# Moving three inverse transforms and their products to other places of a long-convolution and gated-MLP gradient kernel

## The chip, the core and the metric

The kernel runs on one core of one Trainium2 chip. The core has a matrix engine (PE), a vector engine (DVE), a scalar engine (ACT), a general engine (POOL), and a sequencer (SP) that here only issues DMAs; DMAs are issued from SP and from POOL. The metric is the device time of one execution in microseconds.

## The reference

The reference computes a forward pass and the gradients of all its inputs; ten arrays come out. S = 2048 rows, D = 1024 columns, F = 3584, all bf16. Cut to what matters:

```python
def _A_ref(q, k, v, shift_k, ssm_k, ssm_D):        # q is layernorm(x)
    k_shift = sum(k_pad[:, t:t + S] * shift_k[:, 3 - t] for t in range(4))
    kv = k_shift * v
    y = irfft(rfft(kv, 2 * S) * rfft(ssm_k, 2 * S))[:S]   # per column
    return q * (y + kv * ssm_D)

def _B_ref(x, w_gate, w_up, w_down):
    return ((x @ w_gate) * (x @ w_up)) @ w_down

xn = layernorm(x)
out = x + _A_ref(xn, k, v, shift_k, ssm_k, ssm_D) * silu(_B_ref(xn, ...))
# and the gradients of q, k, v, shift_k, ssm_k, ssm_D, w_gate, w_up, w_down
```

The gradient needs the same convolution theorem twice more: with DY the gradient at y, the gradient of kv is the inverse transform of P1 = F(DY) times conj(F(ssm_k)), and the gradient of ssm_k is that of P2 = F(DY) times conj(F(kv)).

## The kernel before

The kernel is written with a tile framework: the code names tiles of pools, and the framework puts in all waits and fixes, when the program is built, the order of instructions on each engine and each DMA queue. It goes by the order of the code as a priority and by a modelled time, so an instruction that is later in the code can be placed ahead of one that the model still sees waiting. On the chip each engine then runs its list strictly in that order. Pools of SBUF are stacked: a pool opened after another was closed takes over its addresses, and a tile of it waits until the last user of those addresses is done. `nc.any.tensor_copy` is put on ACT or DVE by the framework. `dma()` alternates between SP and POOL.

The Fourier transforms are matrix products with twiddle tables of 1024 x 1024 cosines and sines (`twc`, `tws`, held in HBM as TWd and loaded in eight rows of 128 x 1024). Rows of a sequence are split by parity (`sigma` or `par`), columns in two halves (`dh`) of 512. A forward transform (`fwd_transform2`, L226) takes 8 frequency blocks (`gb`), two parities, two halves, and for each 16 matmuls of 128x512 into two PSUM tiles `psA` and `psB`; ACT copies them to SBUF. A spectrum consists of an even part E, an odd part O and, for two of the three, the odd part rotated by a phase (`rotate_O`, L264, four DVE instructions). Products of spectra (`cprod2`, L288) make real and imaginary parts by `csum4` (L272): four multiplications (L278), two sums (L283, L285), and a final sum (L286), each over 128x512 bf16. The two `cprod2` of one (gb, dh) item thus are 28 instructions, of which the imaginary part of the second (7, tag "j") goes to POOL through `eng_i=nc.gpsimd` and 21 to DVE. An inverse transform (`inv_transform2`, L246) takes 8 row blocks (`ub`), two parities and two halves, each 16 matmuls (L256) and one of a single row (L259) into `psI`, and hands the tile to a callback.

The stages in the order of the code, with their tiles:

- H: twiddle tables are made, ssm_k is transposed and transformed, with layer norm and the shifted k beside it; spectra HF go to HBM.
- KV: forward transform of kv (tile KVs), products Y = KVF x HF into the tile YS (64 KB a partition), KVF to HBM (`kv_on_acc`, L475). Y inverse with callback `y_on_out` (L523): writes YFULLd and SOUTd.
- Gate/up: WD is loaded, xn transposed to XNT, then g, u and h = g*u for 28 blocks of F (L551 to L588), written to GTd, UTd, HTd.
- BM: h times w_down, silu and its gradient, writes the output, DYd, DXNAd, DBMd.
- DY: forward transform of DY (`dy_on_acc`, L684), products P1 into the tile YS2, DYF to HBM. Inverse 1 with callback `dkv_on_out` (L741; tiles cb, dyD, dkv, dksh, dv) and, after each of its 8 row blocks, `p2_task` (L765): it loads DYF and KVF, scales DYF on ACT (L774), makes P2 and stores it to HBM. Then P2 is loaded back into YS2, and inverse 2 with `dh_on_out` (L806) transposes its result into DSSMK.
- DBMT: DBM transposed; FG (L839 to L882): for 7 groups of 4 blocks of F, `ps_dh` matmuls, products dgt and dut on DVE, their transposes, then two sets of `ps_dw` matmuls for the weight gradients.
- DWD (L927 to L963): gradient of w_down on PE, with `dk_block` (L888) beside it, which makes the gradients of k and of shift_k on DVE.
- dx (L969 to L1032): gate and up weights transposed (`pst_wt`), then 16 row blocks for each half of D with 56 matmuls `ps_dxn` each; the first half is kept in HALF (f32), the second goes on through the layer-norm gradient.

Of the kernel before, what the change touches and what calls it, by code (L numbers as in the profile page):

```python
# [17 lines left out]
def build_kernel(  # L18
# [71 lines left out]
    DYFd = dram.tile([NB2, P, 4 * D], BF16, name="DYFd")  # L90
    P2d = dram.tile([NB2, P, 4 * D], BF16, name="P2d")
# [217 lines left out]

    def transpose_blocks(pspool, srcs, dst_fn, nblk, tagname):  # L310
# [143 lines left out]

    with tc.tile_pool(name="kvpool", bufs=1) as kvpool, \
            tc.tile_pool(name="twpool_f", bufs=2) as twpool, \
            tc.tile_pool(name="nrows_f", bufs=1) as nrf, \
            tc.tile_pool(name="yspool_f", bufs=1) as yspool:
# [8 lines left out]
        YS = yspool.tile([P, NB2, 2, 2, D], BF16, name="YS")  # L467
        with tc.tile_pool(name="kvf_sb", bufs=2) as kfs, \
                tc.tile_pool(name="kvf_tmp", bufs=1) as ktmp, \
# [5 lines left out]
            def kv_on_acc(sigma, gb, dh, psA, psB):  # L475
                if gb not in kvf_tiles:
                    kvf_tiles[gb] = kfs.tile([P, 3, 2, D], BF16, name="kvf_t")
                    hf_in[gb] = kfs.tile([P, 3, 2, D], BF16, name="hf_in")
                    dma(hf_in[gb][:].rearrange("p a c d -> p (a c d)"), HFd[gb])
                kt = kvf_tiles[gb]  # L480
                ht = hf_in[gb]
# [3 lines left out]
                if sigma == 1:  # L485
                    rotate_O(kt[:, 2, 0, sl], kt[:, 2, 1, sl], kt[:, 1, 0, sl], kt[:, 1, 1, sl], gb, ktmp)
                    Ek = (kt[:, 0, 0, sl], kt[:, 0, 1, sl])
                    Ok = (kt[:, 1, 0, sl], kt[:, 1, 1, sl])
                    Eh = (ht[:, 0, 0, sl], ht[:, 0, 1, sl])
                    Oh = (ht[:, 1, 0, sl], ht[:, 1, 1, sl])  # L490
                    Orh = (ht[:, 2, 0, sl], ht[:, 2, 1, sl])
                    cprod2(YS[:, gb, 0, 0, sl], YS[:, gb, 0, 1, sl], Ek, Eh, False, Ok, Orh, False, ktmp, "yp")
                    cprod2(YS[:, gb, 1, 0, sl], YS[:, gb, 1, 1, sl], Ek, Oh, False, Ok, Eh, False, ktmp, "yp", eng_i=nc.gpsimd)
                    if dh == DH - 1:
                        dma(KVFd[gb], kt[:].rearrange("p a c d -> p (a c d)"))
                        del kvf_tiles[gb]
                        del hf_in[gb]

            def kv_on_nyq(sigma, dh, psN):
                sl = slice(dh * 512, (dh + 1) * 512)  # L500
                nc.scalar.copy(out=KNb[0:1, sigma, sl], in_=psN[:])
                if sigma == 1:
# [10 lines left out]
                    if dh == DH - 1:  # L513
                        nc.sync.dma_start(out=KVFNd[:, :], in_=KNb[:].rearrange("o s d -> o (s d)"))

            fwd_transform2(KVs, lambda b: load_tw_row(twpool, b), fps, kv_on_acc, kv_on_nyq)

        with tc.tile_pool(name="yi_sb", bufs=3) as ysb, \
                tc.tile_pool(name="yi_xn", bufs=2) as yxn, \
                tc.tile_pool(name="ips", bufs=2, space=bass.MemoryType.PSUM) as ips:  # L520
            xn_tiles = {}

            def y_on_out(par, ub, dh, ps):  # L523
                key = (par, ub)
                if dh == 0:
                    xn_tiles[key] = yxn.tile([P, D], BF16, name="xn_l")
                    dma(xn_tiles[key][:], par_rows(XNd, par, ub))
                sl = slice(dh * 512, (dh + 1) * 512)
                yb = ysb.tile([P, 512], BF16, name="yb")
                nc.scalar.copy(out=yb[:], in_=ps[:])  # L530
                kvD = ysb.tile([P, 512], BF16, name="kvD")
                nc.vector.tensor_tensor(kvD[:], KVs[:, par, ub, sl], Dbc[:, sl], ALU.mult)
                yfull = ysb.tile([P, 512], BF16, name="yfull")
                nc.vector.tensor_tensor(yfull[:], yb[:], kvD[:], ALU.add)
                dma(par_rows(YFULLd, par, ub, sl), yfull[:])
                sout = ysb.tile([P, 512], BF16, name="sout")
                nc.vector.tensor_tensor(sout[:], xn_tiles[key][:, sl], yfull[:], ALU.mult)
                dma(par_rows(SOUTd, par, ub, sl), sout[:])
                if dh == DH - 1:
                    del xn_tiles[key]  # L540

            inv_transform2(YS, YN, lambda b: load_tw_row(twpool, b), ips, y_on_out)

    twbase.release()

    wdp = tc.alloc_tile_pool(name="wd_pool", bufs=1, side="right")
    WD = wdp.tile([P, FC, D], BF16, name="WD")
    for fc in range(FC):
        dma(WD[:, fc, :], B_w_down[fc * P:(fc + 1) * P, :])

    with tc.tile_pool(name="xnt_pool", bufs=1) as xtp:  # L551
# [9 lines left out]
        with tc.tile_pool(name="wslab", bufs=2) as wsl, \  # L561
                tc.tile_pool(name="gu_sb", bufs=3) as gus, \
                tc.tile_pool(name="gu_ps", bufs=2, space=bass.MemoryType.PSUM) as gps:
            for fg in range(FG):
# [4 lines left out]
                for fi in range(4):  # L569
                    fc = fg * 4 + fi  # L570
                    for sq in range(SQ):
# [16 lines left out]
                        dma(HTd[rs, cs], h_b[:])  # L588

# [71 lines left out]
    with tc.tile_pool(name="yspool_b", bufs=1) as yspool, \  # L661
            tc.tile_pool(name="nrows_b", bufs=1) as nrb, \
            tc.tile_pool(name="twpool_b", bufs=2) as twpool:
        YS = yspool.tile([P, NB2, 2, 2, D], BF16, name="YS2")
        YN = nrb.tile([1, 2, D], BF16, name="YNb")
        dypool = tc.alloc_tile_pool(name="dypool", bufs=1)
# [4 lines left out]
        with tc.tile_pool(name="dyf_sb", bufs=2) as dfs, \  # L671
# [431 lines left out]
```

## Time and profile before

| quantity | value |
| --- | --- |
| median of 4 runs | 3579.45 us (3576.46 to 3580.23) |
| profiled execution, its own time | 3576.46 us |
| span of the profiled execution | 3574.7 us |
| mean granted PE clock | 0.893 of full speed |
| moved by DMA over the span | 582.86 MB, 163 GB/s |
| PE idle in the KV stage until ACT has copied `kvf_t` | 91.4 us |

The span runs from the first to the last instruction; what lies around it is 1.8 us. Busy time is the time in which at least one instruction of an engine runs. Matmuls are pipelined: one lasts 379 ns, but the next starts well before its end, so PE's pace is read from starts or from a whole stage. The table of stages gives busy time, the granted clock and the DMA traffic for stretches of the span; the starts of stages in it are read from the first and last matmul of each PSUM tile. A line such as L256 or L278 is that of a helper that several stages share; the tiles named beside it tell the stages apart.

### The profile page before, as it was taken

What the parts mean: (1) busy time and instruction counts of PE and PEld (TensorE: products, weight loads), DVE (VectorE), ACT (ScalarE), POOL (GpSimd) and SP (SyncE); (2) the same over time, 40 slices, a digit from 0 to 9 for tenths busy, and PEclk for the clock granted to TensorE, in tenths of its full rate; (3) what the DMA queues carried; (4) which work ended last, traced back from release to release, by engine and by line L of the source; (5) the groups of instructions that cost most, each with busy time, mean ns of one, the idle gap of its engine ahead of it and who ended that gap; (6) DMA issues with size and microseconds to landing.
All of it is one profiled execution on the core that took longest, in us unless ns stands there. A gap on an engine that the chain in (4) does not pass through costs nothing. (4 is left out here: it accounts for less than half of the span.)

```text
span 3574.7 us, 39595 instructions
## 1 busy us (share of the span) xinstructions
PE 2834.9 (79%) x13811; PEld 1299.8 (36%) x14074; DVE 1528.6 (43%) x3373; ACT 1086.4 (30%) x2849; POOL 1091.9 (31%) x1281
## 2 busy tenths in 40 slices
PE   5945459699999976454444969999999899699798
PEld 2412224344443322121111444444444344444443
DVE  7979973111115547686663032222222651100244
ACT  6411101433321111111111454444444444510432
POOL 2237742122232329866662010010010220011021
PEclk9977779799999988777766979999999999799799
DMA  7773254443447742333444063333342873455486
GB/s 268 285 256 121 88 196 144 143 161 139 162 146 244 265 177 89 106 121 141 158 174 170 30 240 116 110 114 121 119 127 99 298 247 124 152 144 160 140 242 183
DMA packets 327911, 582.86 MB, mean 163 GB/s; under 512 B 144655, under 2 KB 195855, under 8 KB 318236
## 3 DMA queue, kind: packets, MB, share of 16 engines
q1 hardware_dynamic: 250350, 292.42, 25.3%
q0 software_dynamic: 77360, 287.89, 22.3%
q8 instruction: 110, 1.80, 0.2%
q14 instruction: 91, 0.75, 0.1%
HBM read 379.62 MB, written 204.77 MB: 163 GB/s over the span
## 5 line engine op out<-in xcount | busy, mean ns | idle before, releaser
L256 PE MATMUL psI<-YS,twc_t 128*128 128x512 bf16 x754 | 309.5, 411 | 266.1 <-ACT cb L750 156.4
L1000 PE MATMUL ps_dxn<-WGT,dgt_l 128*128 128x512 bf16 x890 | 338.4, 380 | 1.8
L577 PE MATMUL psU<-XNT,wu_s 128*128 128x512 bf16 x888 | 337.8, 380 | 1.5
L576 PE MATMUL psG<-XNT,wg_s 128*128 128x512 bf16 x868 | 330.6, 381 | 9.1 <-DMA wg_s<-in_B_w_gate_dram 5.3
L1000 PE MATMUL ps_dxn<-WUT,dut_l 128*128 128x512 bf16 x862 | 327.6, 380 | 0.6 <-ACT WUT L317 0.4
L256 PE MATMUL psI<-YS,tws_t 128*128 128x512 bf16 x748 | 304.1, 407 | 8.4 <-DVE YS L286 7.3
L877 PEld LDWEIGHTS <-XNR 128*128 128x128 bf16 x1792 | 174.4, 98 | 206.9 <-issue 2.0
L862 PE MATMUL ps_dh<-DBMT,WDT 128*128 128x512 bf16 x861 | 205.9, 380 | 4.6 <-ACT DBMT L317 2.6
L256 PEld LDWEIGHTS <-tws_t 128*128 128x128 bf16 x768 | 79.1, 103 | 347.4 <-issue 280.7
L955 PE MATMUL ps_dwd<-DBM,HH 128*128 128x512 bf16 x868 | 202.2, 380 | 3.1 <-ACT wd_b L960 0.8
L608 PE MATMUL ps_bm<-WD,ht_t 128*128 128x512 bf16 x877 | 195.5, 379 | 5.8 <-DMA ht_t<-HTd 4.8
L583 DVE TENSOR_TENSOR h_b<-g_b,u_b 128x512 bf16<-128x512 bf16 x112 | 47.6, 425 | 352.1 <-ACT u_b L581 352.1
L877 PE MATMUL ps_dw<-DG,XNR 128*128 128x512 bf16 x875 | 196.2, 379 | 2.3 <-ACT DG L317 1.2
L877 PE MATMUL ps_dw<-DU,XNR 128*128 128x512 bf16 x879 | 193.6, 379 | 0.9
L242 PE MATMUL psA<-KV,twc_t 128*128 128x512 bf16 x245 | 100.4, 413 | 91.4 <-ACT kvf_t L483 91.4
L880 ACT CAST w_b<-ps_dw 128x512 bf16<-128x512 f32 x112 | 65.6, 585 | 295.1 <-PE ps_dw L877 292.2
L317 DVE COPY WDT<-pst_fg 128x128 bf16<-128x128 bf16 x81 | 17.9, 224 | 316.9 <-PE pst_fg L315 309.3
L579 ACT CAST g_b<-psG 128x512 bf16<-128x512 f32 x112 | 65.5, 585 | 276.4 <-PE psG L576 266.8
L278 POOL TENSOR_TENSOR p1j_m<-da_t,hf_in 128x512 bf16<-128x512 bf16 x64 | 139.9, 2206 | 26.3 <-ACT da_t L692 13.7
L243 PE MATMUL psB<-DY,tws_t 128*128 128x512 bf16 x256 | 102.3, 400 | 55.7 <-DMA tws_t<-TWd 54.2
L68 POOL DMA_DIRECT2D out_dram<-w_b x56 | 30.4, 542 | 361.1 <-ACT w_b L880 316.4
L608 PEld LDWEIGHTS <-ht_t 128*128 128x128 bf16 x896 | 86.0, 98 | 121.6 <-issue 15.7
(332 smaller groups left out, 5299.2 us busy)
## 6 DMA issues: line engine op xcount, KB each, us to landing
dgt_l<-DGTd SPq DMA_DIRECT2D x32, 896.0 KB, 5.6
dut_l<-DUTd POOLq DMA_DIRECT2D x32, 896.0 KB, 8.4
hf_in<-HFd SPq DMA_DIRECT2D x16, 1536.0 KB, 7.4
kt<-KPAD SPq DMA_DIRECT2D x64, 256.0 KB, 5.4
kt<-KPAD POOLq DMA_DIRECT2D x64, 256.0 KB, 5.7
ut_t<-UTd POOLq DMA_DIRECT2D x28, 512.0 KB, 7.2
gt_t<-GTd SPq DMA_DIRECT2D x28, 512.0 KB, 5.7
DGTd<-dgt SPq DMA_DIRECT2D x28, 512.0 KB, 3.0
```

The costliest lines, as they stand in the source:

```text
L242: nc.tensor.matmul(psA[:], twc_t[:, ub * P:(ub + 1) * P], rhs, start=(ub == 0), stop=(ub == NB2 - 1))
L243: nc.tensor.matmul(psB[:], tws_t[:, ub * P:(ub + 1) * P], rhs, start=(ub == 0), stop=(ub == NB2 - 1))
L256: nc.tensor.matmul(ps[:], tws2[c][:, gb * P:(gb + 1) * P], Pspec[:, gb, par, c, dh * 512:(dh + 1) * 512], start=first, stop=False)
L278: e.tensor_tensor(m[:], a, b, ALU.mult)
L576: nc.tensor.matmul(psG[:], wg_s[:, dc, fi * P:(fi + 1) * P], rhs, start=(dc == 0), stop=(dc == DC - 1))
L577: nc.tensor.matmul(psU[:], wu_s[:, dc, fi * P:(fi + 1) * P], rhs, start=(dc == 0), stop=(dc == DC - 1))
L608: nc.tensor.matmul(ps[:, dh * 512:(dh + 1) * 512], lhsT, WD[:, fc, dh * 512:(dh + 1) * 512], start=(fc == 0), stop=(fc == FC - 1))
L862: nc.tensor.matmul(ps[:], WDT[:, ddc, fi * P:(fi + 1) * P], DBMT[:, ddc, cs], start=(ddc == 0), stop=(ddc == DC - 1))
L877: nc.tensor.matmul(ps[:], XNR[:, sb, dc * P:(dc + 1) * P], src[:, sb, :], start=(sb == 0), stop=(sb == NB - 1))
L880: nc.scalar.copy(out=w_b[:], in_=ps[:])
L955: nc.tensor.matmul(pss[k][:, dh * 512:(dh + 1) * 512], HH[:, sb, fi * P:(fi + 1) * P], DBM[:, sb, dh * 512:(dh + 1) * 512], start=(sb == 0 ...
L1000: nc.tensor.matmul(ps[:], lt[:, fc, :], wt[:, fc, :], start=(i_acc == 0), stop=(i_acc == n_acc - 1))
```

## The change

- KV: products are no longer split; all 28 instructions of an item run on DVE (`eng_i` isn't given any more). They go to a small tile `ystg` and from there to HBM (Yd). `GB_IN = NB2` makes this hold for all 8 blocks, so that the list of Y items for the gate/up stage (`y_items`) is empty.
- The Y inverse runs after gate/up and before BM. WD is loaded after gate/up in the code, just ahead of it. The callback loads its part of xn and kv itself.
- DY: the forward transform only copies and stores DYF; no HF is loaded. XNR is loaded ahead of DY in the code.
- P1: 16 items (`product_pass_item`), each two loads, 28 DVE instructions and a store, are placed by `p1_tick` along the 28 blocks of FG. Inverse 1 follows FG; DBM is loaded after it in the code.
- P2: 16 items, with the scaling on ACT, are placed by `p2_tick` along the 32 row blocks of dx; inverse 2 comes last in the kernel. HALF becomes bf16.
- The inverses are `inv_transform2h`: the half `dh` is the outer loop, a half of the spectrum is loaded from HBM (tile YSh, two buffers), and all twiddle rows are loaded once for each half.
- DBM's pool no longer overlaps in time with that of DBMT and XNR.

The core of the diff:

```diff
+    def y_products(dst2, kt3, ht3, pool, tag):
...
+        cprod2(dst2[:, 0, 0, :], dst2[:, 0, 1, :], Ek, Eh, False, Ok, Orh, False, pool, tag)
+        cprod2(dst2[:, 1, 0, :], dst2[:, 1, 1, :], Ek, Oh, False, Ok, Eh, False, pool, tag)
...
+    def product_pass_item(kind, gb, dh, io_pool, tmp_pool):
+        sl = slice(dh * 512, (dh + 1) * 512)
+        out_t = io_pool.tile([P, 2, 2, 512], BF16, name=f"pp_out_{kind}")
...
+        elif kind == "P1":
+            dt = io_pool.tile([P, 2, 2, 512], BF16, name="pp_dyf")
+            dma(dt[:], DYFv[gb, :, :, :, sl])
+            ht = io_pool.tile([P, 3, 2, 512], BF16, name="pp_hf")
+            dma(ht[:], HFv[gb, :, :, :, sl])
+            p1_products(out_t, dt, ht, tmp_pool, "pp1")
+            dma(P1v[gb, :, :, :, sl], out_t[:])
...
+    def make_pass_scheduler(kind, io_pool, tmp_pool, total_slots):
+        items = [(gb, dh) for gb in range(NB2) for dh in range(DH)]
...
+        def tick(i, final=False):
+            target = len(items) if final else min(len(items), (len(items) * (i + 1) + total_slots - 1) // total_slots)
+            while state["done"] < target:
...
+    def inv_transform2h(Psrc_v, PNsrc, tw_pool, ys_pool, nr_pool, pspool, on_out, side_task=None):
...
+        for dh in range(DH):
+            sl = slice(dh * 512, (dh + 1) * 512)
+            first_tw = load_tw_row(tw_pool, 0)
+            YSh = ys_pool.tile([P, NB2, 2, 2, 512], BF16, name="YSh")
+            for gb in range(NB2):
+                dma(YSh[:, gb, :, :, :], Psrc_v[gb, :, :, :, sl])
+            for ub in range(NB2):
+                twc_t, tws_t = first_tw if ub == 0 else load_tw_row(tw_pool, ub)
...
+                for par in range(2):
...
+                    on_out(par, ub, dh, ps)
...
-                    cprod2(YS[:, gb, 0, 0, sl], YS[:, gb, 0, 1, sl], Ek, Eh, False, Ok, Orh, False, ktmp, "yp")
-                    cprod2(YS[:, gb, 1, 0, sl], YS[:, gb, 1, 1, sl], Ek, Oh, False, Ok, Eh, False, ktmp, "yp", eng_i=nc.gpsimd)
+                    if gb < GB_IN:
+                        ht = hf_in[gb]
+                        ystg = yst.tile([P, 2, 2, 512], BF16, name="ystg")
+                        y_products(ystg, kt[:, :, :, sl], ht[:, :, :, sl], ktmp, "yp")
+                        dma(Ydv[gb, :, :, :, sl], ystg[:])
...
-            inv_transform2(YS, YN, lambda b: load_tw_row(twpool, b), ips, y_on_out)
...
+        inv_transform2h(Ydv, YNd, ytw, yys, ynr, ips, y_on_out)
...
-                    cprod2(YS[:, gb, 0, 0, sl], YS[:, gb, 0, 1, sl], Ed, Eh, True, Od, Oh, True, dtmp, "p1")
-                    cprod2(YS[:, gb, 1, 0, sl], YS[:, gb, 1, 1, sl], Ed, Orh, True, Od, Eh, True, dtmp, "p1", eng_i=nc.gpsimd)
...
-            inv_transform2(YS, YN, lambda b: load_tw_row(twpool, b), ips, dkv_on_out, side_task=p2_task)
...
-            inv_transform2(YS, YN, lambda b: load_tw_row(twpool, b), ips, dh_on_out)
...
+            p1_tick = make_pass_scheduler("P1", p1io, p1tmp, FG * 4)
...
+                    p1_tick(fg * 4 + fi)
...
+        inv_transform2h(P1v, P1Nd, i1tw, i1ys, i1nr, ips, dkv_on_out)
...
-        HALF = hfp.tile([P, NB, 512 * max(DH - 1, 1)], F32, name="HALF")
+        HALF = hfp.tile([P, NB, 512 * max(DH - 1, 1)], BF16, name="HALF")
+        p2_tick = make_pass_scheduler("P2", p2io, p2tmp, DH * NB)
...
+                p2_tick(dh * NB + sb)
...
+        inv_transform2h(P2v, P2Nd, i2tw, i2ys, i2nr, ips, dh_on_out)
```

More of the change, by code (lines that the diff above doesn't have):

```diff
@@ L496, in kv_on_acc @@
                         del kvf_tiles[gb]
-                        del hf_in[gb]
+                        if gb in hf_in:
+                            del hf_in[gb]
             def kv_on_nyq(sigma, dh, psN):
```

404 lines of the change are left out of this document (225 added, 179 removed).

## The prediction

> **What bounds the kernel now.** I read the page first, then busy time by stage, then who waits for whom, then single instructions in order of time.
>
> ```profile
> span 3574.7 us, 39595 instructions
> PE 2834.9 (79%) x13811; PEld 1299.8 (36%) x14074; DVE 1528.6 (43%) x3373; ACT 1086.4 (30%) x2849; POOL 1091.9 (31%) x1281
> PE   5945459699999976454444969999999899699798
> ```
>
> The span lies 1.8 us under this execution's own 3576.46 us; the median of the runs is 3 us above that. No engine is full over the whole span. PE is at 9 tenths in most of the 40 slices and at 4 to 6 in two valleys, slices 3 to 6 and 16 to 22, counted from 1. The table of stages puts names to them (columns: us, PE, PEld, DVE, ACT and POOL busy with counts, granted PE clock, DMA share, GB/s):
>
> ```profile
> 65.00:190.00 125.00, 116.45 (x518) 51.65 (x527) 116.93 (x319) 66.72 (x122) 33.53 (x56) 0.99 0.81 292
> 246.00:467.00 221.00, 125.24 (x501) 53.07 (x511) 219.35 (x332) 33.55 (x64) 163.93 (x112) 0.78 0.30 110
> 467.00:507.00 40.00, 10.35 (x34) 3.36 (x34) 40.00 (x75) 0.75 (x2) 19.22 (x17) 0.61 0.24 92
> 507.00:628.00 121.00, 118.68 (x504) 48.13 (x514) 37.82 (x98) 18.62 (x32) 32.26 (x60) 0.97 0.55 194
> 628.00:664.00 36.00, 14.86 (x128) 11.24 (x125) 7.87 (x35) 24.60 (x95) 6.08 (x10) 0.57 0.42 131
> 664.00:1060.00 396.00, 387.50 (x1756) 175.87 (x1792) 47.60 (x112) 120.25 (x224) 95.77 (x174) 0.99 0.40 147
> 1060.00:1298.00 238.00, 222.69 (x937) 89.76 (x956) 121.64 (x182) 34.39 (x33) 71.72 (x134) 1.00 0.69 236
> 1298.00:1328.00 30.00, 12.71 (x29) 2.92 (x30) 7.48 (x13) 2.16 (x4) 6.40 (x12) 0.60 0.82 303
> 1328.00:1533.00 205.00, 122.27 (x509) 52.44 (x519) 159.02 (x292) 34.85 (x66) 184.15 (x110) 0.80 0.27 96
> 1533.00:1567.00 34.00, 5.29 (x17) 1.58 (x16) 34.00 (x52) 0.17 (x1) 20.36 (x19) 0.62 0.20 78
> 1567.00:1872.00 305.00, 147.26 (x519) 56.33 (x529) 207.47 (x436) 47.24 (x60) 192.76 (x162) 0.73 0.44 154
> 1872.00:1936.00 64.00, 10.95 (x27) 3.69 (x27) 30.35 (x50) 4.27 (x4) 26.64 (x30) 0.55 0.64 246
> 1936.00:2067.00 131.00, 126.92 (x631) 55.35 (x643) 0.61 (x2) 55.94 (x155) 4.86 (x9) 0.97 0.11 37
> 2067.00:2112.00 45.00, 18.39 (x145) 14.43 (x146) 10.40 (x49) 25.13 (x99) 11.20 (x21) 0.53 0.86 323
> 2112.00:2784.00 672.00, 653.82 (x3719) 322.91 (x3790) 174.09 (x620) 296.72 (x933) 65.99 (x123) 1.00 0.36 117
> 2784.00:3075.00 291.00, 269.05 (x1460) 118.89 (x1489) 120.90 (x215) 140.36 (x451) 54.19 (x100) 0.98 0.59 211
> 3104.00:3340.00 236.00, 214.92 (x1080) 107.15 (x1098) 16.42 (x69) 45.31 (x159) 26.99 (x20) 0.92 0.55 154
> 3374.00:3564.00 190.00, 188.60 (x861) 85.73 (x876) 80.46 (x105) 53.20 (x76) 37.83 (x43) 1.00 0.73 215
> ```
>
> In order these are: H forward transform, KV forward with the Y products (two rows), Y inverse, XNT transposes, gate/up matmuls, BM, the DY boundary, DY forward with the P1 products, their tail, inverse 1 with the P2 products, reload of P2, inverse 2, DBMT transposes, FG, DWD, and the two halves of dx. FG, gate/up, BM and dx are full of PE work. The valleys are the product stages: there DVE is busy throughout (219 of 221) or POOL is (184 of 205, 193 of 305).
>
> ```profile
> ACT cb L750 <- DVE dkv L754: 199.2, 15, 25.7
> PE psI L256 <- ACT cb L750: 156.4, 14, 24.8
> PE psA L242 <- ACT kvf_t L483: 91.4, 6, 21.2
> PE psB L243 <- DMA tws_t<-TWd: 57.6, 3, 33.7
> PE psI L256 <- DVE YS L286: 57.2, 9, 21.8
> PE psI L256 <- DMA YS<-P2d: 55.2, 4, 37.8
> ```
>
> PE waits for evictions, which wait for DVE; for products that aren't finished; for twiddle rows whose issue stands on POOL behind products; and for P2's reload. Why DVE is so slow there shows in single instructions (start, duration):
>
> ```profile
> 280.13 0.41 DVE L285 TENSOR_TENSOR ypr_s<-ypr_m,ypr_m 128x512 bf16<-128x512 bf16 x1
> ...
> 284.82 0.41 DVE L286 TENSOR_TENSOR YS<-ypr_s,ypr_s 128x512 bf16<-128x512 bf16 x1
> ...
> 300.16 1.37 DVE L286 TENSOR_TENSOR YS<-ypr_s,ypr_s 128x512 bf16<-128x512 bf16 x1
> 301.45 3.95 DVE L278 TENSOR_TENSOR ypi_m<-kvf_t,hf_in 128x512 bf16<-128x512 bf16 x3
> ```
>
> The second row is the 14th instruction after the first: one starts every 0.335 us. At 300 us, where POOL works on its share (`ypj`), the next one starts 1.29 us later.
>
> **The change, part by part.** Every product goes to DVE alone; Y, P1 and P2 pass through HBM; the three inverses move behind the gate/up stage, FG and dx, each as two half-width passes; P1 and P2 products run inside FG and dx.
>
> *KV and XNT.* Each of 16 (gb, dh) items now has 28 DVE products: 28 x 0.335 = 9.4 us. The rotation is four instructions; on the undisturbed H stage its first and the instruction behind its last are
>
> ```profile
> 97.27 0.48 DVE L266 TENSOR_SCALAR rot_t<-hf_t,C 128x512 f32<-128x512 bf16 x1
> ...
> 99.39 0.15 DVE L419 RECIPROCAL rr<-r 128x1 f32<-128x1 f32 x1
> ```
>
> so 2.1 us. 16 x 11.5 = 184 us: products end at about 250 + 184 + 6 of waits = 440 instead of 507. PE needs 125 us of those and is still held by `kvf_t`'s two buffers. Its last gb starts when the products of the one two before are done, 440 - 46 = 394, and takes 125/8 = 16: it ends near 410. XNT (36 us) needs only KV's memory; it can end at 446 if its copies go to ACT, or at 476 if it starts behind the products. I take 465, nearer the second, because gate/up's evictions need memory of the last products: **gate/up starts 199 us earlier**. If the rate didn't change, DVE would need the old 261 us.
>
> *Y inverse.* It starts after 396 us of gate/up, at 861. Its half of Y (4.2 MB) can only be loaded where XNT lay, once gate/up is over: 14 us at 303 GB/s plus 3 of latency, 17. PE restarts at half pace, as here over ten matmuls:
>
> ```profile
> 1693.52 0.58 PE L256 MATMUL psI<-YS,twc_t 128*128 128x512 bf16 x1 [12.69 <-ACT cb L750]
> ...
> 1697.73 0.50 PE L256 MATMUL psI<-YS,twc_t 128*128 128x512 bf16 x1
> ```
>
> Ten starts take 4.2 us; at gate/up's pace (396 us for 1792) they take 2.2: 2 us lost. The matmuls stay: 544 at the pace of the 504 in 121 us, less a little for records missing, 128. Traffic beside it: 8 for contention. WD's load has the gate/up stage to hide in; without that cover, 7.3 MB cost 24 us. BM starts at 861 + 17 + 2 + 128 + 8 = 1016, not 1060: **-44**.
>
> *DY forward.* XNR (4.2 MB) now comes ahead of DY, while two `hf_in` loads (3.1 MB) go: +4 on the boundary. Without products the stage resembles the H transform's 125 us for the same matmuls; I take 122, so -83. **-79** together.
>
> *534 us go*: tail 34, inverse 1 305, reload 64, inverse 2 131.
>
> *DBMT*: 14.5 MB moved in 45 us. DBM and DSSMK (8.4 MB) leave it; 6.1 MB are 19 us. Between 19 and 45 I take 32: **-13**.
>
> *FG* gains 16 P1 items: 150 us of DVE beside its 174 of 672. What that costs PE no row shows directly. Bounds: zero, or inverse 1's loss with 8 side tasks of two items, (305 - 131)/16 = 10.9 us an item. The nearest row is DWD, where 16 `dk_block` tasks fill DVE for 121 us and PE is idle 22 of 291, mostly at its start. **+10.**
>
> *Inverse 1*, after FG: 17 + 2 + 128, and 15 for traffic = **+162**. It streams three loads and two stores per 4 us group.
>
> *dx*: 16 P2 items, 150 us of DVE, beside 97 of 426; the scaling stays as many ACT instructions as before. dx's DMA share is already 0.55 and 0.73. **+15.** The bf16 HALF changes the type of an eviction; ACT has room (45 of 236), nothing.
>
> *Inverse 2* at the very end: 17 + 2 + 131 = **+150**. The tail behind PE was 11 us of layer norm and becomes copies and stores: same.
>
> Sum: -44 - 79 - 534 - 13 + 10 + 162 + 15 + 150 = -333; 3576 - 333 = **3243 us**.
>
> For the traffic terms the rows are:
>
> ```profile
> YS<-P2d SPq DMA_DIRECT2D x4, 1024.0 KB, 8.9
> hf_in<-HFd SPq DMA_DIRECT2D x16, 1536.0 KB, 7.4
> DMA to landing us min/median/max: 2.7/3.1/11.1
> L68 POOL DMA_DIRECT2D KVFd<-kvf_t x8: 542/582/585, 279.2 to 501.3; - x8
> ```
>
> (The third is that of `tws_t`.) Inverse 1 moves in its first half 16 groups x 0.66 MB, 4.2 of twiddles and 4.2 of the next half of P1: 18.9 MB in 64 us, 295 GB/s. The highest rate of a stage is 323, so it fits; at the 246 of the P2 reload it takes 77 us, 13 more, and at the 194 of the old Y inverse 97, 33 more. The Y inverse needs 16.8 MB there, 262 GB/s. I charge 15 and 8, near the 246 case. The Trainium skill ("DMA: Bandwidth & Descriptors", its opening table) gives about 358 GB/s per core for HBM; by that the half needs 53 us, the two charges vanish, and the sum would be 3220.
>
> The Trainium skill ("SBUF — State Buffer", "SBUF: two separate sides") also speaks against putting more on DVE: a DMA issued by POOL, about 620 ns alone, takes about 3100 beside a DVE operation that uses both ports. The last row above doesn't show that here: POOL's issues took 542 to 585 ns in a stage with DVE full. By that rule the items' 48 POOL issues would be 2.5 us longer each, an estimate of 119 us on POOL, and 3362 if all of it reached PE; as a rival from rows it stands below.
>
> **The rivals.**
> - *The inverses become bound by transfers.* A twiddle row now serves two groups, 8 us, not four, and must land in that time; the slowest landing was 11.1. If all rows of the Y inverse and inverse 1 are that late: 32 x 3.1 = 99, less the 23 charged: **3319**. For it: 295 GB/s wanted. Against: a median of 3.1.
> - *Side work holds up its engine.* Half the items cost what they cost in inverse 1: 16 x 10.9 = 174, less 25: **3392**. For it: ACT waiting 199 us for `dkv`. Against: there POOL was in the chain too.
> - *POOL's issues are held up by DVE's work.* The items issue 96 DMAs, 48 of them on POOL. The slowest kind of issue there is
>
> ```profile
> L68 POOL DMA_DIRECT2D dut_l<-DUTd x32 | 49.9, 1561 | 259.8 <-PE ps_dxn L1000 235.7 <-PE ps_dwd L955 13.0 <-issue 11.0
> ```
>
>   At 1.56 us instead of 0.58 they cost 47 if PE waits for each: **3290**. Against it: 0.58 beside a full DVE.
> - *The change doesn't do what it says*: DVE stays slow for another reason than POOL. The KV stage keeps its 261 us, 67 more: **3310**.
> - *Slower*: each item stands in front of PE's copies on DVE's queue with its whole time and the landing of its load, 9.4 + 7.4 = 16.8 us; 32 x 16.8 = 538, less 25: **3756**. Place: DVE's queue in FG and dx. It turns slower from (333 + 25)/32 = 11.2 us an item. Against it: by the sums above DVE stays idle for four tenths or more of both stages.
>
> **How the numbers follow.** Forecast 0.58, transfers 0.19, side work 0.12, POOL's issues 0.03, no relief 0.04, slower 0.04. The forecast's own range: down to 3144 if the three load stalls (51), both traffic charges (23) and the side charges (25) are all hidden, up to 3310. The other cases of the same sign lie in reach, so the range is 3144 to 3392. Faster by over 0.2% 0.95, within 0.2% (about what a measurement of this kernel can tell from no change) 0.01, slower 0.04.
>
> **What would show it.** Right: products on DVE starting every 0.33 us in KV and none on POOL; gate/up near 465; DY forward near 122 us; three inverses of 130 to 145 us with a load stall ahead of each; FG and dx within 25 us of 672 and 460. Wrong: waits of PE on `twc_t`/`tws_t` in the inverses (transfers); waits on DVE for `DG`, `DU` or `dgt` in FG, or on `dgt_l` in dx (side work); products still at 1.3 us.

## The result, and the profile after

| kernel | median, us | runs | ratio to before, 95% interval |
| --- | --- | --- | --- |
| before | 3579.26 (3575.40 to 3584.40) | 13 | 1 |
| after | 3197.27 (3187.93 to 3204.02) | 8 | 0.8933 [0.8924, 0.8943] |

The change takes 382 us away. The forecast was 3243, 46 us more than measured; its range was 3144 to 3392. First the page of the kernel after, the same lines as were shown of before:

```profile
span 3191.4 us, 40101 instructions
PE 2803.5 (88%) x13809; PEld 1293.4 (41%) x14074; DVE 1351.6 (42%) x3580; ACT 1098.3 (34%) x2978; POOL 638.6 (20%) x1085
PE   4948759999899997949999999989899778979988
DMA packets 396404, 645.84 MB, mean 202 GB/s; under 512 B 149140, under 2 KB 255636, under 8 KB 391845
```

The wide valley (slices 16 to 22 of before) is gone; what is left of it are single slices between stages. PE's busy time is nearly the same, 2804 instead of 2835, so nearly all of the gain is PE's idle time. DVE now does all products and is still busy for less time than before, 1352 instead of 1529; POOL lost 453. The price is traffic: 63 MB more in a shorter span.

The table of stages of the kernel after (us, then PE, PEld, DVE, ACT, POOL busy with counts, granted PE clock, DMA share, GB/s):

```profile
244.00:399.00 155.00, 120.24 (x501) 51.96 (x509) 149.88 (x414) 33.11 (x63) 12.01 (x21) 0.88 0.62 218
399.00:445.00 46.00, 15.42 (x129) 12.03 (x128) 37.97 (x106) 28.32 (x130) 9.86 (x16) 0.55 0.68 235
445.00:836.00 391.00, 387.80 (x1756) 175.77 (x1792) 48.27 (x114) 119.60 (x223) 95.81 (x174) 0.99 0.41 149
836.00:850.00 14.00, 0.07 (x1) 0.10 (x1) 0.43 (x1) 0.81 (x2) 8.13 (x12) 0.68 0.91 322
850.00:979.00 129.00, 125.88 (x533) 50.86 (x544) 37.05 (x93) 18.73 (x32) 40.37 (x76) 0.98 0.68 222
979.00:1215.00 236.00, 224.15 (x937) 90.53 (x956) 121.04 (x181) 33.33 (x32) 71.72 (x134) 0.99 0.68 236
1215.00:1249.00 34.00, 14.46 (x37) 3.50 (x38) 8.53 (x15) 3.99 (x6) 10.74 (x20) 0.65 0.94 336
1249.00:1360.00 111.00, 110.01 (x501) 49.82 (x510) 93.64 (x281) 34.27 (x65) 15.80 (x23) 1.00 0.72 244
1360.00:1418.00 58.00, 18.06 (x145) 14.73 (x146) 40.80 (x131) 27.59 (x124) 11.65 (x19) 0.53 0.86 292
1418.00:2090.00 672.00, 654.38 (x3719) 322.90 (x3791) 192.62 (x673) 301.09 (x965) 70.17 (x130) 1.00 0.37 124
2090.00:2106.00 16.00, 8.55 (x29) 3.24 (x31) 0.76 (x2) 0.23 (x2) 5.97 (x9) 0.89 0.98 365
2106.00:2236.00 130.00, 121.53 (x506) 48.60 (x513) 47.13 (x124) 18.52 (x32) 55.30 (x103) 0.96 0.80 276
2236.00:2559.00 323.00, 283.35 (x1559) 129.74 (x1589) 142.12 (x287) 161.10 (x525) 60.81 (x107) 0.93 0.66 226
2559.00:2797.00 238.00, 212.94 (x1012) 101.83 (x1030) 138.47 (x419) 60.58 (x161) 41.09 (x40) 0.92 0.79 241
2847.00:3037.00 190.00, 188.57 (x861) 85.72 (x876) 80.50 (x105) 53.18 (x76) 37.83 (x44) 1.00 0.73 220
3037.00:3057.00 20.00, 11.65 (x29) 3.71 (x30) 4.25 (x6) 3.76 (x6) 5.57 (x8) 0.66 0.99 358
3057.00:3184.00 127.00, 124.21 (x632) 54.63 (x642) 0.30 (x1) 56.86 (x159) 9.69 (x18) 1.00 0.27 87
```

In order: KV until its last matmul; XNT; gate/up; the wait ahead of the Y inverse; Y inverse; BM; the DY boundary; DY forward; DBMT; FG; the load of P1; inverse 1; DWD; the two halves of dx; the load of P2; inverse 2. The profiled execution took 3193 us (its span plus 1.8). Its steps beside those of the forecast:

| step | forecast | measured | difference |
| --- | --- | --- | --- |
| gate/up starts at | 465 | 445 | -20 |
| gate/up | 396 | 391 | -5 |
| Y inverse, its load and restart | 155 | 14 + 129 | -12 |
| BM | 238 | 236 | -2 |
| DY boundary and forward | 34 + 122 | 34 + 111 | -11 |
| DBMT | 32 | 58 | +26 |
| FG with P1's items | 682 | 672 | -10 |
| inverse 1, load and restart | 162 | 16 + 130 | -16 |
| DWD | 320 | 323 | +3 |
| dx with P2's items | 475 | 478 | +3 |
| inverse 2, load and restart | 150 | 20 + 127 | -3 |
| tail | 11 | 7 | -3 |

The differences add up to -50, which is 3243 less 3193. One step went against the forecast and is clearly wrong: DBMT. FG's figure hides a second error, since P1's items are hardly in FG: the first P1 product runs at 1273 us and the last at 1461. So 13 of the 16 items are done beside the DY forward transform and DBMT, and the last three in FG's first 43 us. The framework placed them there, ahead of the code's order. What that did to DBMT shows in who waited for whom from 1250 to 1420 us (engine, tile, line, releaser: us, times, longest), and in SP's list of instructions there:

```profile
POOL pp_dyf L68 <- DVE pp1i_m L282: 34.5, 4, 9.4
PE pst_db L418 <- DMA dbm_l<-DBMd: 28.5, 6, 16.2
```

```profile
1357.91 0.53 SPq L68 DMA_DIRECT2D pp_dyf<-DYFd  x1
...
1367.31 0.53 SPq L68 DMA_DIRECT2D pp_hf<-HFd  x1
1368.13 0.86 SPq L68 DMA_DIRECT2D dbm_l<-DBMd  x2
```

PE waits 28.5 us for DBM's rows. SP issues the first of them only at 1368, right behind a load of a P1 item that had to wait for the item's buffer, 8 us after DY forward ended. The forecast for DBMT went by bytes alone; it didn't ask whose DMAs would stand ahead in the lists.

The product stage itself is as forecast. DVE's instructions in KV of the kernel after (start, duration):

```profile
301.15 0.42 DVE L287 TENSOR_TENSOR ypr_s<-ypr_m,ypr_m 128x512 bf16<-128x512 bf16 x1
...
302.16 0.42 DVE L290 TENSOR_TENSOR ystg<-ypr_s,ypr_s 128x512 bf16<-128x512 bf16 x1
```

The second row is the third instruction after the first: one starts about every 0.335 us, at the time where it was 1.29 in the kernel before. The last KV product ends at 437 us (forecast 440).

### The profile page after: what moved, and what is told of

The parts are those of the page before. It is cut to its first block, busy times and chain, and to the rows that moved or that the text cites. A ratio compares the mean times of both kernels' runs of the same rounds, so it can differ in the third digit from the quotient of the medians.

```text
span 3191.4 us, 40101 instructions
## 1 busy us (share of the span) xinstructions
PE 2803.5 (88%) x13809; PEld 1293.4 (41%) x14074; DVE 1351.6 (42%) x3580; ACT 1098.3 (34%) x2978; POOL 638.6 (20%) x1085
## 5 line engine op out<-in xcount | busy, mean ns | idle before, releaser
L405 PE MATMUL psI<-YSh,twc_t 128*128 128x512 bf16 x756 | 295.0, 390 | 39.6 <-DMA tws_t<-TWd 14.0
L405 PE MATMUL psI<-YSh,tws_t 128*128 128x512 bf16 x745 | 289.5, 389 | 0.7 <-issue 0.2
L1061 PEld LDWEIGHTS <-dgt_l 128*128 128x128 bf16 x896 | 88.5, 99 | 113.9 <-DMA dgt_l<-DGTd 7.9
L661 PEld LDWEIGHTS <-wg_s 128*128 128x128 bf16 x896 | 87.9, 98 | 114.1 <-issue 9.3
L1061 PEld LDWEIGHTS <-dut_l 128*128 128x128 bf16 x896 | 88.5, 99 | 110.4 <-DMA dut_l<-DUTd 3.6
L420 ACT COPY HH<-pst_hh 128x128 bf16<-128x128 bf16 x416 | 110.3, 265 | 64.0 <-PE pst_hh L418 52.3
L662 PEld LDWEIGHTS <-wu_s 128*128 128x128 bf16 x896 | 87.9, 98 | 108.0 <-DMA wu_s<-in_B_w_up_dram 1.7
```

Source lines behind the costliest of these rows:

```text
L405: nc.tensor.matmul(ps[:], tws2[c][:, gb * P:(gb + 1) * P], YSh[:, gb, par, c, :], start=first, stop=False)
L661: nc.tensor.matmul(psG[:], wg_s[:, dc, fi * P:(fi + 1) * P], rhs, start=(dc == 0), stop=(dc == DC - 1))
L662: nc.tensor.matmul(psU[:], wu_s[:, dc, fi * P:(fi + 1) * P], rhs, start=(dc == 0), stop=(dc == DC - 1))
L1061: nc.tensor.matmul(ps[:], lt[:, fc, :], wt[:, fc, :], start=(i_acc == 0), stop=(i_acc == n_acc - 1))
```

## The experiments

The theory: DVE was slowed by POOL's share of the products, and once that is gone the moved products and inverses fit beside PE's work. Its first rival: the gain is the moving itself (the items leave the path, whichever engine makes them). Two kernels separate these. A second question, further down, is whether the P2 items cost dx DVE's time or their traffic.

**b_nopool: before, with every product on DVE and nothing moved.**

```diff
-                    cprod2(YS[:, gb, 1, 0, sl], YS[:, gb, 1, 1, sl], Ek, Oh, False, Ok, Eh, False, ktmp, "yp", eng_i=nc.gpsimd)
+                    cprod2(YS[:, gb, 1, 0, sl], YS[:, gb, 1, 1, sl], Ek, Oh, False, Ok, Eh, False, ktmp, "yp")
... (the same for "p1" in DY and "p2" in inverse 1)
```

> The kernel before with its products all on DVE and nothing moved (eng_i dropped at three places). Theory 1, POOL's share slows DVE fourfold and that alone made the valleys: the KV products end near 440 us instead of 507 (-67), DY forward and its tail take about 160 us instead of 239 (bound by 16 x 9.4 us of DVE, -79), inverse 1 about 205 us instead of 305 (-100); about 3330 us. Theory 2, the new places of products and inverses made the gain: 28 instead of 21 instructions per item on DVE in the same places, so no gain or a loss, 3579 us or more.

Measured 3342.88, ratio 0.9329 [0.9314, 0.9345]. One argument, deleted at three places, takes 236 of the 382 us. The KV products end at 439 us (440 expected). Its stages DY forward and inverse 1:

```profile
1261.00:1390.00 129.00, 116.57 (x517) 51.34 (x518) 128.63 (x386) 34.55 (x65) 8.64 (x16) 0.96 0.44 161
1405.00:1650.00 245.00, 139.20 (x518) 53.23 (x518) 188.60 (x557) 47.24 (x60) 36.35 (x68) 0.78 0.58 206
```

and a wait in inverse 1:

```profile
ACT cb L750 <- DVE dkv L754: 137.1, 14, 22.3
```

DY forward falls from 205 us to 129 with DVE full throughout. Its tail falls from 34 us to 15, so the two take 144 us where about 160 were expected; the products, 9.4 us an item, run on until 1419, into inverse 1. Inverse 1 falls from 305 only to 245, not to the 205 expected, since its evictions (`dkv` on DVE) still stand behind whole P2 items in DVE's list. That, the reload (54) and the tails are what moving takes away.

**a_pool: after, with POOL's share put back.**

```diff
-        cprod2(dst2[:, 1, 0, :], dst2[:, 1, 1, :], Ek, Oh, False, Ok, Eh, False, pool, tag)
+        cprod2(dst2[:, 1, 0, :], dst2[:, 1, 1, :], Ek, Oh, False, Ok, Eh, False, pool, tag, eng_i=nc.gpsimd)
... (the same in p1_products and p2_products)
```

> The kernel after with POOL's share of the products restored in all three product functions (7 of 28 instructions per item). Theory 1: the KV products end 60 to 67 us later, and P1 and P2 items take POOL about 11 us each, partly hidden, with POOL's DMA issues behind them; 3270 to 3350 us. Theory 2: where the products stand is what counts, so 3190 to 3210 us.

Measured 3474.49, ratio 0.9708 [0.9694, 0.9723]: POOL's share costs 277 us, more than the theory had said. Seen from all four kernels: it costs 236 in the old places and 277 in the new; moving the work brings 105 with it and 146 without. KV's products end at 514 us instead of 437, 77 later where 60 to 67 were expected. In one stretch of KV both rates stand side by side. DVE and then POOL, whose list has been waiting for a load until 306.77:

```profile
306.33 0.42 DVE L289 TENSOR_TENSOR ypi_s<-ypi_m,ypi_m 128x512 bf16<-128x512 bf16 x1
306.66 0.42 DVE L282 TENSOR_TENSOR ypr_m<-kvf_t,hf_in 128x512 bf16<-128x512 bf16 x1
...
308.67 0.42 DVE L289 TENSOR_TENSOR ypr_s<-ypr_m,ypr_m 128x512 bf16<-128x512 bf16 x1
309.01 1.38 DVE L270 TENSOR_SCALAR rot_t<-kvf_t,C 128x512 f32<-128x512 bf16 x1
310.31 1.37 DVE L290 TENSOR_TENSOR ystg<-ypr_s,ypr_s 128x512 bf16<-128x512 bf16 x1
```

```profile
306.77 3.33 POOL L282 TENSOR_TENSOR ypj_m<-kvf_t,hf_in 128x512 bf16<-128x512 bf16 x1 [10.48 <-DMA hf_in<-HFd]
310.06 1.33 POOL L290 TENSOR_TENSOR ystg<-ypj_s,ypj_s 128x512 bf16<-128x512 bf16 x1
```

DVE starts one every 0.33 us until 309.01. POOL's first instruction starts at 306.77, beside them, and lasts 3.33 us instead of 1.33: it ends at 310.10, when DVE has gone from its products to the rotation. From then on the two alternate: POOL's second instruction ends at 311.39, and DVE's, which started at 310.31, ends 0.29 us later, at 311.68. These rows fit turns of whole instructions rather than a shared rate. The Trainium skill ("SBUF — State Buffer", "Who interferes with whom") says the same: a DVE instruction with two SBUF inputs and a POOL instruction that reads SBUF exclude each other for the whole instruction. By that rule a product on POOL costs DVE its whole length, and the rows agree: while the two alternate, DVE starts one every 1.29 to 1.30 us instead of 0.335, so about 0.955 us go to POOL's.

This price accounts for the KV stage of the kernel before, as an estimate from these rows. Its 16 x 7 = 112 products on POOL cost DVE 112 x 0.955 = 107 us, and DVE's own work is 16 x (21 x 0.335 + 2.1) = 146 us. The sum is 253 us; the stage took 261.

In the new places POOL's share does a second harm. Waits of PE in dx of this kernel, 2772 to 3079 us:

```profile
PE ps_dxn L1061 <- DMA dgt_l<-DGTd: 46.1, 5, 14.1
```

Half the loads of dx are issued by POOL, in order behind its products. The load of the longest of these waits is issued at 2846.09, behind a POOL product that took 7.28 us, and PE goes on at 2855. In the kernel after these waits are 5.9 us. The first half of dx takes 306 us instead of 238; no run splits the other part of these 68 us.

**Where Y's items belong: a_gbin2.** After, with Y items of 6 of 8 blocks in the gate/up stage.

```diff
-    GB_IN = NB2
+    GB_IN = 2
```

> The kernel after with GB_IN = 2: Y products of six of eight blocks (12 items) run in the gate/up stage. Theory 1, KV is still bound by DVE and side items in a stage full of matmuls cost almost nothing: PE ends KV forward near 363 us instead of 399, gate/up still takes 391 to 396 us; about 3162 us. Rival, side items hold up their engine as they did in the old inverse 1, 10.9 us each: 12 x 10.9 = 131 in gate/up, about 3290 us.

Measured 3181.33, ratio 0.8885 [0.8872, 0.8898]: half of the expected gain. KV on PE ends at 363 instead of 398, as expected. But the framework places all 12 items at once in XNT and the first 112 us of gate/up, instead of spreading them. That stretch, here and in the kernel after:

```profile
418.00:530.00 112.00, 96.11 (x418) 42.02 (x419) 94.48 (x281) 27.27 (x51) 31.20 (x51) 0.92 0.88 305
```

```profile
445.00:557.00 112.00, 110.25 (x491) 49.55 (x502) 13.84 (x33) 33.24 (x62) 26.83 (x49) 0.97 0.44 159
```

DMA share 0.88 instead of 0.44, and PE loses 14 us of 112. Gate/up takes 408 us instead of 391: 17 for 12 items, 1.4 each. XNT grows from 36 us to 46.

**P1 where the code puts it: a_p1first.** P1's pools are opened ahead of FG's, so that they take over addresses which only come free later.

```diff
-        with tc.tile_pool(name="fg_big", bufs=1) as fgb, \
+        with tc.tile_pool(name="p1pass_io", bufs=2) as p1io, \
+                tc.tile_pool(name="p1pass_tmp", bufs=1) as p1tmp, \
+                tc.tile_pool(name="fg_big", bufs=1) as fgb, \
```

> The kernel after with the pools of the P1 items opened ahead of those of FG, so that they lie over DY's tile and no P1 item can run before DY forward has ended; inverse 1's first half then lies over P1's memory. Theory 1, in the kernel after the P1 items ran in DY forward and their DMAs stood ahead of DBMT's loads, and inverse 1's load stall is only a matter of addresses: DBMT takes about 40 us instead of 58, the stall goes from 16 to 2, FG stays within 10 us of 672; about 3165 us. Rival, items that run in FG hold it up by up to 10.9 us each: 3197 - 32 + 174 = 3339 us. If DBMT's time has another cause, 3183 us.

Measured 3189.99, ratio 0.8908 [0.8895, 0.8921]. Its stages DBMT and FG:

```profile
1359.00:1395.00 36.00, 17.65 (x163) 14.86 (x162) 12.47 (x62) 24.53 (x100) 7.50 (x13) 0.62 0.59 183
1395.00:2075.00 680.00, 661.43 (x3776) 321.25 (x3774) 301.78 (x983) 304.50 (x1000) 83.33 (x145) 0.99 0.47 158
```

DBMT takes 36 us instead of 58, so 22 of its 26 us over the forecast were P1's items. FG now has them (DVE 302 instead of 193) and takes 8 us longer: 0.5 us an item, for 9.4 us of DVE work each. Of the 22 won, 8 go there and 6 to inverse 1, whose load stall grew from 16 us to 22 although P1 had been in HBM for hundreds of microseconds. The stall isn't P1's lateness.

**a_p1split: the stall ahead of inverse 1.** As a_p1first, with the two buffers of YSh as two pools of one, in all three inverses.

```diff
-            YSh = ys_pool.tile([P, NB2, 2, 2, 512], BF16, name="YSh")
+            YSh = ys_pool[dh].tile([P, NB2, 2, 2, 512], BF16, name="YSh")
...
-    with tc.tile_pool(name="i1_ys", bufs=2) as i1ys, \
+    with tc.tile_pool(name="i1_ys", bufs=1) as i1ysa, \
+            tc.tile_pool(name="i1_ysb", bufs=1) as i1ysb, \
...
```

> As a_p1first, and the two buffers of YSh in the three inverses become two pools of one buffer each. In a_p1first the loads of inverse 1's half still started only when FG's last matmul was done, at 2075.9 us. Theory 1, a tile waits for everything that lies under its whole pool, so 64 KB a partition reached into FG's own tiles: with 32 KB pools inverse 1's first half lies over P1's memory alone, is loaded during FG, and the stall from FG's last matmul to the first cb of inverse 1 goes from 22 to about 6 us: about 3174 us. Rival, what holds the loads is the order of the DMA queues behind FG's stores: no change, 3190 us.

Measured 3179.55, ratio 0.8881 [0.8868, 0.8895]. From FG's last matmul to the first eviction `cb` of the inverse, 2079.4 to 2089.1, 9.7 us instead of 22. A first half of P1 that no longer shares a pool with the second can be loaded while FG still uses what lies under the second: its loads are issued from 1586 us on, during FG. So this stall is a matter of which addresses a pool covers. The other two stalls stayed, 14 us ahead of the Y inverse and 20 ahead of inverse 2, although their pools were split too; only where Y's and P2's pools are also opened first (a_best2, below) do they fall. FG took 686 us here, which gives 6 of the gain back. It took 684 to 688 us in a_best2, a_best3 and a_best5 as well, where P1's half is also loaded during FG; in what way that costs PE, no run shows.

**What P2 costs dx: its loads or its products?** dx's first half grew from 220 us to 238. Two kernels, each with one half of the items' work (T stands for traffic, V for DVE's time).

a_p2noload:

```diff
-            dma(dt[:], DYFv[gb, :, :, :, sl])
...
-            dma(kt[:], KVFv[gb, :, :, :, sl])
+            dt, kt = p2_keep[dh]        # the two items of gb 0 only are loaded
```

> The kernel after, where the P2 items load DYF and KVF only for the first frequency block and use those tiles for all 16 items, so P2 is not the reference's; their DVE and ACT work and their stores stay. dx's first half takes 238 us from its first ps_dxn matmul to the last HALF copy, 18 more than in the kernel before. Theory T (traffic of the items delays dgt_l and dut_l): 220 to 225 us, and about 3182 us in all. Theory V (DVE and ACT work of the items stands ahead of copies of weights): stays 235 to 240 us, 3197 us.

a_p2nodve:

```diff
-            p2_products(out_t, dt, kt, tmp_pool, "pp2")
-            dma(P2v[gb, :, :, :, sl], out_t[:])
+            nc.vector.tensor_tensor(out_t[:, 0, 0, :], dt[:, 0, 0, :], kt[:, 0, 0, :], ALU.mult)
+            dma(P2v[gb, :, 0, 0, sl], out_t[:, 0, 0, :])
...
```

> The kernel after, where each P2 item keeps its loads, its scaling and the bytes of its store, but makes one product on DVE instead of 28, so P2 is not the reference's. Theory T: dx's first half stays at 235 to 245 us, 3197 us in all. Theory V: 220 to 225 us, about 3182 us.

Measured 3183.92, ratio 0.8896 [0.8878, 0.8913], and 3198.79, ratio 0.8937 [0.8919, 0.8955]. The first half of dx in the kernel before, in a_p2noload and in a_p2nodve:

```profile
3104.00:3324.00 220.00, 207.30 (x1003) 100.49 (x1021) 11.49 (x47) 32.33 (x108) 24.88 (x18) 0.94 0.53 148
```

```profile
2564.00:2789.00 225.00, 208.46 (x1009) 100.66 (x1027) 137.21 (x419) 59.60 (x158) 30.90 (x27) 0.93 0.63 179
```

```profile
2568.00:2806.00 238.00, 210.74 (x1010) 100.81 (x1029) 19.12 (x81) 51.62 (x112) 44.84 (x48) 0.92 0.74 225
```

With all products and hardly any loads it is 225; with all loads and hardly any products it stays at 238. So 13 of the 18 us are the loads, and the 120 us of DVE work cost next to nothing. The medians agree: 13 us under the kernel after, and 2 over it. PE's waits for loads agree too; in the kernel after and in a_p2noload:

```profile
PE ps_dxn L1061 <- DMA dgt_l<-DGTd: 5.9, 3, 4.4
PE pst_wt L418 <- DMA wnat<-in_B_w_up_dram: 3.2, 1, 3.2
PE ps_dxn L1061 <- DMA dut_l<-DUTd: 3.0, 2, 1.8
```

```profile
PE ps_dxn L1065 <- DMA dgt_l<-DGTd: 1.5, 1, 1.5
PE ps_dxn L1065 <- DMA dut_l<-DUTd: 1.1, 1, 1.1
```

12.1 us became 2.6; in a_p2nodve, with the loads, they are 15.3. In the kernel before PE waited for none of them there. The longer landing of `dgt_l` (median 5.6 us before, 9.2 after) is no evidence: before, SP issued all of them, and 9.2 is that of those which POOL now issues; `dut_l`, always issued by POOL in the kernel before, took 8.4 there. a_p2noload still has 9.0.

**All of it with four blocks: a_best2.** GB_IN = 4, Y, P1 and P2 pools first, YSh split.

```diff
+    GB_IN = 4
+    with tc.tile_pool(name="ypass_io", bufs=2) as ypio, \
+            tc.tile_pool(name="ypass_tmp", bufs=1) as yptmp, \
+            tc.tile_pool(name="xnt_pool", bufs=1) as xtp:
...
+    with tc.tile_pool(name="p2pass_io", bufs=2) as p2io, \
+            tc.tile_pool(name="p2pass_tmp", bufs=1) as p2tmp, \
+            tc.tile_pool(name="wt_pool", bufs=1) as wtp, \
```

> The kernel after with GB_IN = 4 (KV then has 34 us of rotations and 75 us of products on DVE, under PE's 118), the pools of the Y, P1 and P2 items opened ahead of their stages' other pools, and YSh in two pools. Theory 1: KV and XNT 36 us earlier, gate/up 5 to 17 us longer, DBMT 22 shorter, FG 9 longer, and three load stalls of 14, 16 and 20 us mostly gone (-40): about 3120 us. Rival, side items and early loads take the gain back in the stages they move to: 3165 us or more.

Measured 3188.81, ratio 0.8899 [0.8879, 0.892]. The stalls did shrink: from the last matmul of the stage ahead to the first of the Y inverse 5 us instead of 14, and to the first eviction of inverse 2 11 instead of 20. But the gain was given back, as the rival said: KV ended 12 us earlier, but gate/up started at 468 instead of 445, with the Y items now in XNT; dx's first half took 249 us instead of 238. Which of the edits did it, no run separates.

**Fewer buffers: a_p2buf1 and a_best4.** Can loads that run ahead be held back by one buffer instead of two?

```diff
-            tc.tile_pool(name="p2pass_io", bufs=2) as p2io, \
+            tc.tile_pool(name="p2pass_io", bufs=1) as p2io, \
```

> The kernel after with one buffer instead of two for the tiles of the P2 items, so that an item's loads can't run while the item before computes: the same bytes over a longer time. If the traffic at the start of dx delays dgt_l and dut_l (as the run without P2's loads showed, 225 us for the first half instead of 238), the first half falls to 225 to 232 us, about 3187 us in all. Rival, the bytes themselves cost it wherever they fall: 236 to 240 us, 3197 us; or the items reach into the second half and hold up the layer-norm gradient there: over 3205 us.

Measured 3243.41, ratio 0.9053 [0.9034, 0.9073]: the opposite. dx's first half and ACT's wait in it:

```profile
2572.00:2852.00 280.00, 229.23 (x1028) 104.20 (x1027) 146.25 (x442) 60.89 (x147) 41.97 (x41) 0.87 0.72 210
```

```profile
ACT pp_dyf L370 <- DMA pp_dyf<-DYFd: 180.9, 14, 18.4
```

With one buffer an item's load can't start before the item ahead is done. The scalings of the items stand in ACT's list and wait 181 us for loads, and behind them stand evictions and copies that PE needs. This fits the rival of side work that holds up its engine. The same wait in the kernel after, over its 238 us:

```profile
ACT pp_dyf L370 <- DMA pp_dyf<-DYFd: 61.4, 7, 12.5
```

With two buffers the loads are early for more of the items.

> a_best3 with one buffer instead of two for the tiles of the Y items and of the P2 items. If traffic of hurried side items costs 17 us in gate/up and 13 in dx and slower items cost less: about 3140 to 3150 us. Rival, no difference to a_best3: 3164 us.

a_best4 is a_best3 (below) with one buffer for Y's and P2's items. Measured 3237.22, ratio 0.9036 [0.9023, 0.905]. Gate/up took 440 us instead of a_best3's 408, dx's first half 275 instead of 237. The expectation was wrong in the same way at both places.

**a_best3: GB_IN = 2, P1's pools first, YSh split.** The three edits shown above, nothing else.

> The kernel after with GB_IN = 2, the pools of the P1 items ahead of FG's, and YSh in two pools. If the two gains measured apart (16 and 17 us) are in different stages and add: about 3164 us. Rival, they meet in one resource: 3175 us or more.

Measured 3163.89, ratio 0.8835 [0.8822, 0.8848], as expected: the 16 us of a_gbin2 and the 18 of a_p1split add up. It beats both kernels, the kernel after by 33 us.

**a_best5: is it ACT's wait in dx?** a_best3, with the scaling of P2 moved from ACT's work in the items into the eviction of inverse 2 (only the items of the first frequency block keep one).

```diff
-            for a in range(2):
-                nc.scalar.activation(dt[:, a, :, :], dt[:, a, :, :], ACT.Identity, scale=wc[:])
+            for a in range(2 if gb == 0 else 0):
+                nc.scalar.activation(dt[:, a, :, :], dt[:, a, :, :], ACT.Identity, scale=whalf0[:])
...
-            nc.scalar.copy(out=hb[:], in_=ps[:])
+            nc.scalar.activation(hb[:], ps[:], ACT.Copy, scale=4.0 / L)
```

> a_best3 with the P2 items' scaling taken off ACT: the factor 4/L goes into inverse 2's eviction (a copy becomes a scaled copy), only the two items of the first frequency block keep a scaling (by one half in one row), and the Nyquist row is scaled to match. In a_best3 ACT waits 77 us in order for the items' DYF loads, and dx's first half takes 237 us; the run without loads took away the traffic and this wait together. If ACT's wait is the cause: 225 to 229 us for the first half, about 3153 us in all. If the traffic is the cause, or the products' own wait on DVE takes the place: 235 to 240 us, 3164 us.

Measured 3203.84, ratio 0.8952 [0.8937, 0.8967]. The wait is gone from dx and dx is slower:

```profile
2547.00:2804.00 257.00, 217.82 (x1023) 102.21 (x1021) 136.11 (x405) 36.28 (x146) 41.20 (x39) 0.89 0.88 223
```

```profile
PE ps_dxn L1065 <- DMA dgt_l<-DGTd: 22.5, 4, 14.5
```

The DMA share is 0.88 instead of a_best3's 0.80, and PE waits for `dgt_l`, once as long as 14.5 us. So taking ACT's wait away doesn't bring dx's 18 us back. Nor does it explain the 13 us of a_p2noload, though the expectation took it that the wait was gone there. In that kernel the scalings wait as long as in the kernel after (61.4 us), for DVE instead of for loads, and yet dx's first half takes 225 us:

```profile
ACT pp_dyf L376 <- DVE pp2i_m L282: 64.6, 10, 7.9
```

What made a_best5's dx slower isn't shown. Perhaps ACT's wait had also held the next items' loads back, so that they now come closer together; that is a reading, and no run shows it. Whether the bytes do it alone, or the order that the framework gives to the lists, stays open: every edit changes both.

## Why the prediction was right, and where it was off

**The mechanism: right, and shown.** The forecast had "products on DVE starting every 0.33 us in KV"; measured are 0.335, and one trace (a_pool) has both rates with POOL's arrival between them. The rival that DVE was slow for another reason fell with b_nopool, which changes only the engine.

**The sum: closer than its terms.** Nine of the twelve steps in the table above were forecast 2 to 20 us too dear, 82 in all, and three too cheap, 32 in all. That DBMT's error runs against the others is luck.

**KV and XNT, 199 forecast, 219 measured.** The products end at 437, near the 440 forecast. The mis-sized term is XNT. I had it end at 446 or 476 and took 465 for gate/up; it ran from 402 to 438, beside KV's last products, and gate/up waited only 8 us more.

**Y inverse, inverse 1, inverse 2: 31 us too dear in sum.** The stalls ahead of them took 14, 16 and 20 us; the forecast had 17 for each load and 2 for PE's restart. For inverse 1 and 2 PE does wait for `YSh` (8.0 and 8.8 us, in several pieces). Ahead of the Y inverse it waits for something else:

```profile
PE psI L405 <- DMA tws_t<-TWd: 14.0, 1, 14.0
```

This is the first twiddle row. POOL issues it only at 845.07, after a wait of 5.46 us for the last stores of `h_b`. So there the forecast's size was near by luck, and its cause, the load of Y's half, was not what ended the wait. The charges for traffic, 8 and 15, were too high: the inverses took 129 and 130 us with a DMA share of 0.68 and 0.80, where 128 was the price without traffic. The case of no charge was nearly right: the 276 GB/s of inverse 1 went through with a loss of 2 us.

**DY: 11 us better than forecast.** I took 122 from the H transform's row; it took 111. The H transform had 292 GB/s beside it instead of 244 and twice ACT's work, so it was a poor model; which of the two made it slow was not tried.

**DBMT: this step failed.** "6.1 MB are 19 us. Between 19 and 45 I take 32" counted bytes alone. It took 58. The placement of P1's items ahead of the code's order put their loads in front of DBM's rows in SP's and POOL's lists; a_p1first, which keeps the items out of that stretch, took 36. The description of the framework ahead of the forecast says that "an instruction that is later in the code can be placed ahead"; the forecast didn't apply this to the items.

**FG, +10 forecast: for the wrong place.** In the kernel after FG has three of the 16 items and no cost (672 as before). Where it has them all (a_p1first) they cost 8; the other 13 cost DBMT 22 us here.

**dx, +15 forecast, +18 measured.** Size right. The runs attribute 13 of the 18 to the loads, not to DVE. The remaining 5 aren't explained; other parts of the change that reach into dx, such as HALF in bf16, were not tried apart.

**The rivals.** Transfers: they didn't bind the inverses, where I had put them, but dx, where I hadn't. Side work that holds up its engine: no cost of it shown in the kernel after, but 46 us when an item's loads come late (a_p2buf1). POOL's issues held up by DVE: not seen; POOL's issues of KVFd took 542 to 558 ns beside a full DVE, and those of `dgt_l` 1564 ns (median) in dx, no more than the 1561 of `dut_l` in the kernel before. So the extra 2.5 us an issue of the forecast's estimate don't appear beside these products. What does hold up POOL's issues is POOL's own products (a_pool). No relief: refuted. Slower: would have needed 11.2 us an item; 0.5 in FG (a_p1first) and about 1.1 in dx were measured.

## What to carry to other kernels

Before moving work, read the starts of one kind of instruction at a time when another engine works and at a time when it doesn't: here that one reading, 0.335 against 1.29 us, held 236 of the 382 us, and three deleted arguments bring them. Here work moved beside a full stage cost little (0.5 to 1.4 us for an item of 9.4) as long as its loads were early, and the price of late ones was paid by whatever stood behind it in the same engine's list. Ask of each moved load whose DMAs it now stands in front of, and where the scheduler rather than the code will put it.

## What was not expected of the hardware

- While a half of YSh was loaded, all DMAs together moved 358 and 365 GB/s at a DMA share of 0.99 and 0.98 for 20 and 16 us, above every stage shown of the kernel before (323 at most). The Trainium skill ("DMA: Bandwidth & Descriptors", its opening table) puts the limit of a core at about 358; these rows lie at it, the higher one 2% above. a_p1split shortened such a stall by an earlier start of the load.
- The exclusion works against POOL as well, and not turn by turn. In a_pool's rows above a POOL instruction of 1.33 us took 3.33. In KV of the kernel before, between 279 and 434 us, POOL came six times with a product into a running series of DVE's products. Each time DVE went on at 0.335 us for another 2.9 to 6.0 us, up to the first instruction of its next rotation (a TENSOR_SCALAR), which took 1.37 us instead of 0.48. The other way round, an instruction of DVE's at 353.88 took 6.20 us while POOL ran five. Why the rotation is where POOL gets in, no run shows.
- A load of 896 KB issued by POOL landed in 8.4 to 9.2 us (medians of the kernels before and after), and one issued by SP in 5.6 (before).
